# Two layers of linear attention and MLP on one core: 64 bytes more in an unused tile

## The chip, the cores and the metric

The kernel runs on one core of a Trainium2 chip. The metric is the device time of one execution in microseconds. The profile is taken from a single execution by the hardware profiler; its span runs from the first to the last instruction of the program.

## The reference

Two layers, each an attention block without softmax followed by an MLP, over 2048 rows of 448 columns in float32 (16 heads of 28):

```
phi = lambda t: jnp.where(t > 0, t + 1, jnp.exp(t)) + 1e-6
def A(x, wqkv, wo):
    q, k, v = heads(x @ wqkv)
    kv = einsum("bhsd,bhse->bhde", phi(k), v)
    z  = einsum("bhsd->bhd", phi(k))
    o  = einsum("bhqd,bhde->bhqe", phi(q), kv) / (einsum("bhqd,bhd->bhq", phi(q), z) + 1e-6)
    return merge(o) @ wo
def B(x, w1, b1, w2, b2):
    return gelu(x @ w1 + b1) @ w2 + b2      # 448 -> 1792 -> 448
for layer in range(2):
    x = x + A(layernorm(x), wqkv, wo)
    x = x + B(layernorm(x), w1, b1, w2, b2)
```

## The kernel before

Precision: each large product is made of float32r matmuls. An operand is split into a high part (a cast copy by ACT) and a low part (the rest, by DVE or POOL), and the product is high x high, high x low and low x high, all added into the same PSUM bank. Of the last 64 of the 448 rows of a contraction, high and low parts are stacked into one operand of 128 partitions, so that two matmuls do instead of three.

Staging: a layer has two parts. Phase 1 goes over 16 tiles of 128 rows: layer norm, transpose, the k and q projections (`proj`, L306 to L311), phi, and the accumulation of G (L481 to L485, normalised x against phi(k), four banks). A transition then forms z, the kv matrix and its product with wo (L621, L641, L651), in plain float32. Phase 2 goes over four blocks of four tiles. For each of 14 slices of 128 hidden columns, `mlp1` makes the first MLP product: 11 matmuls that write 128 x 512 (L801 to L805); slices of w1 are stationary and the block's normalised, transposed x (`XH`, `XL`) is moving. ACT makes g by gelu and gh by a cast copy, DVE gl. `mlp2` makes the second product: for each of the block's four tiles 3 matmuls that write 128 x 448 (L819 to L821); gh or gl is stationary and a slice of w2 is moving. The attention part of the next block is put between (L743 to L747 among it).

A matmul of TensorE is preceded by a weight load of its own: the stationary operand's 128 columns are read from SBUF (row PEld, LDWEIGHTS), and then the moving operand's columns are read and streamed through.

Order: the kernel is written under a manual schedule, so each engine's instructions stand in the order of the program; TensorE works through one list.

Memory: tiles come from pools and are given addresses in SBUF in the order in which their tags are first used, one behind the other. The address is the byte offset within each of the 128 partitions. What matters here, in order, with the start of the first buffer modulo 256 bytes as the built program has it:

- pool `consts` (`ones` and `ident` at 128), pool `wts`: w1h, w1l, w1x, w2h, w2l, all at 64; their slices begin at multiples of 256 bytes from there
- pool `work`, first tags: nine x tiles at 64, five halves `S` of 4096 bytes at 64 (staging, transposed squares, Mh and part of Ml), the twelve small tiles of the layer norm's statistics (bst, bmv, bve, brs, 32 bytes each)
- the unused tile `space`, L912, 128 bytes
- then `tail`, the tags W (wk, pq and others), `XH`, `XL`, V (wq), A (gh, qh, xnh), B (gl, ql, xnl), e (g, phi), E and F (kh, kl, qh, ql), xn, and the small dn and rd. All of these but the small ones start at 64 modulo 256.

Nothing ever writes or reads `space`; it sets where the tiles behind it lie. The lines around it:

```
    stage_a(0, 0)
    work.tile([128, 32], F32, name="space", tag="space", bufs=1)
    bn = ln_bn(xt[0, 1])
    stage_n(0, 0)
```

`stage_a` is what first allocates the statistics' tiles, `stage_n` what first allocates `tail`.

Of the kernel before, what the change touches and what calls it, by code (L numbers as in the profile page):

```python
# [9 lines left out]
F32 = mybir.dt.float32  # L10
# [12 lines left out]
def linear_attn_mlp_kernel(  # L23
# [28 lines left out]
    work = ctx.enter_context(tc.tile_pool(name="work", bufs=2))  # L52
# [138 lines left out]
    def ln_bn(xs):  # L191
        st = work.tile([128, 6], F32, name="bst", tag="bst", bufs=3)
        dve.bn_stats(st, xs)  # L193
        return st
# [182 lines left out]
    def stage_a(l, t):  # L377
        sts[l, t] = ln_stats(xt.pop((l, t)))
# [530 lines left out]


    stage_a(0, 0)
    work.tile([128, 32], F32, name="space", tag="space", bufs=1)  # L912
    bn = ln_bn(xt[0, 1])
    stage_n(0, 0)
    split_hi("k", 0, st_k)
# [4 lines left out]
    for l in range(LAYERS):  # L920
# [27 lines left out]
        for tok in ORDER.split():  # L948
            name, j = tok.rstrip("0123456789"), int("0" + tok.lstrip("abcdefghijklmnopqrstuvwxyzQTG"))
# [69 lines left out]
```

## Time and profile before

| | us |
|---|---|
| median of 3 runs | 878.83 (878.70 to 878.84) |
| the profiled execution's own time | 877.81 |
| its span | 876.1 |
| TensorE: matmuls busy, in the span | 870.8 |
| first MLP product (L801 to L805), 1232 matmuls, start to start | 281.5 |
| second MLP product (L819 to L821), 1344 matmuls, start to start | 272.3 |
| other float32r matmuls, start to start | 291.3 |

The first three rows are measured times. In a profile, PE is TensorE's matmul stream and PEld its weight loads, which run beside it. Matmuls overlap in their pipeline, so the duration of one (365 ns at 448 columns, 391 ns at 512) is longer than the distance between two starts (about 203 and 227 ns); for the rate of the stream the distance counts. "Start to start" in the table is the sum of these distances over all matmuls of the lines named.

### The profile page before, as it was taken

To read this page: it belongs to the slowest core of one execution; us is meant where nothing else is said; L and a number is where in the kernel's file an instruction comes from. 1 tells how busy PE (TensorE), PEld (TensorE's weight loads), DVE (VectorE), ACT (ScalarE), POOL (GpSimd) and SP (SyncE) were. 2 spreads that over 40 slices of the span, in tenths; PEclk is the share of its full clock that TensorE was granted. 3 is DMA by queue.
4 is the path that set the end of the run, shared out by engine and by line. 5 is a ranking of instruction groups with operands and counts; after the bars stand their busy time and mean duration, and the time that the engine had idled before them with its cause. 6 is when DMAs were issued, how large, how long until landed. Compare 5 with 4: busy or idle time off the path is not lost.

```text
span 876.1 us, 11676 instructions
## 1 busy us (share of the span) xinstructions
PE 870.8 (99%) x4182; PEld 771.5 (88%) x4182; DVE 489.0 (56%) x953; ACT 343.3 (39%) x603; POOL 220.8 (25%) x250
## 2 busy tenths in 40 slices
PE   9999999999999999999999999999999999999998
PEld 8999888888888888888899998888888888888887
DVE  6877585658455443226477875864674483433112
ACT  5676635324323322333356565332233133223221
POOL 5566532335013102012222344110220140140000
PEclk9999999999999999999999999999999999999999
DMA  5475636633413402051146543352332423111001
GB/s 159 134 228 173 198 88 207 188 96 122 132 59 105 156 0 97 1 179 49 48 135 195 164 128 106 103 181 81 109 110 91 128 76 115 49 49 42 1 1 43
DMA packets 63482, 94.76 MB, mean 108 GB/s; under 512 B 8896, under 2 KB 58560, under 8 KB 63424
## 3 DMA queue, kind: packets, MB, share of 16 engines
q1 hardware_dynamic: 63424, 94.01, 34.5%
q8 instruction: 33, 0.54, 0.3%
q14 instruction: 25, 0.20, 0.1%
HBM read 56.17 MB, written 34.60 MB: 104 GB/s over the span
## 4 chain that ended last, share of the span: by engine, by line
PE 98%; DVE 0%; DMA 0%; POOL 0%; ACT 0%; issue 0%; DVEq 0%
PE y L821 10%; PE y L819 10%; PE y L820 10%; PE hp L802 9%; PE hp L803 9%; PE hp L801 9%; PE hp L805 3%; PE hp L804 3%; PE psk L307 2%; PE G L482 2%; PE psq L306 2%; PE psq L307 2%; PE psq L308 2%; PE G L481 2%; PE G L483 2%; PE psk L308 2%
## 5 line engine op out<-in xcount | busy, mean ns | idle before, releaser
L811 DVE TENSOR_TENSOR gl<-g,gh 128x512 fp32r<-128x512 f32 x112 | 83.4, 745 | 299.8 <-ACT gh L810 299.8
L807 ACT ACTIVATE g<-hp,b1s 128x512 f32<-128x512 f32 x112 | 77.1, 689 | 406.5 <-PE hp L805 403.3
L821 PE MATMUL y<-w2h,gl 128*128 128x448 f32 x448 | 163.7, 365 | 0.0
L820 PE MATMUL y<-w2l,gh 128*128 128x448 f32 x448 | 163.6, 365 | 0.0
L819 PE MATMUL y<-w2h,gh 128*128 128x448 f32 x448 | 163.6, 365 | 0.0
L802 PE MATMUL hp<-XH,w1l 128*128 128x512 f32 x336 | 131.5, 391 | 0.0
L801 PE MATMUL hp<-XH,w1h 128*128 128x512 f32 x336 | 131.2, 391 | 0.0
L803 PE MATMUL hp<-XL,w1h 128*128 128x512 f32 x336 | 131.2, 391 | 0.0
L203 POOL TENSOR_TENSOR brs<-bve,mhalf 128x1 f32<-128x1 f32 x64 | 39.5, 618 | 284.6 <-DVE bve L201 276.5
L819 PEld LDWEIGHTS y<-w2h,gh 128*128 128x128 f32 x448 | 84.1, 188 | 9.0
L820 PEld LDWEIGHTS y<-w2l,gh 128*128 128x128 f32 x448 | 84.1, 188 | 8.4
L821 PEld LDWEIGHTS y<-w2h,gl 128*128 128x128 f32 x448 | 84.2, 188 | 6.6
L803 PEld LDWEIGHTS hp<-XL,w1h 128*128 128x128 f32 x336 | 63.1, 188 | 14.1 <-issue 0.6
L802 PEld LDWEIGHTS hp<-XH,w1l 128*128 128x128 f32 x336 | 63.1, 188 | 11.3
L801 PEld LDWEIGHTS hp<-XH,w1h 128*128 128x128 f32 x336 | 63.1, 188 | 10.9
L810 ACT CAST gh<-g 128x512 fp32r<-128x512 f32 x112 | 69.6, 622 | 3.6
L694 POOL TENSOR_TENSOR pz<-pq,zb 128x448 f32<-128x448 f32 x32 | 36.7, 1150 | 87.2 <-DVE dn L700 71.3
L416 POOL TENSOR_TENSOR xnl<-x,xnh 128x384 fp32r<-128x384 f32 x32 | 35.1, 1097 | 70.0 <-ACT xnh L415 37.9
L296 DVE TENSOR_TENSOR XL<-sp,XH 128x512 fp32r<-128x512 f32 x50 | 42.9, 864 | 4.2 <-ACT XH L295 4.2
L805 PE MATMUL hp<-XL,w1x 128*128 128x512 f32 x112 | 43.6, 389 | 0.0
L804 PE MATMUL hp<-XH,w1x 128*128 128x512 f32 x112 | 43.6, 389 | 0.0
L193 DVE BATCH_NORM_STATS2 bst<-x 128x6 f32<-128x448 f32 x64 | 39.9, 624 | 4.8 <-DMA x<-in_A_x_dram 3.7
(146 smaller groups left out, 1565.0 us busy)
## 6 DMA issues: line engine op xcount, KB each, us to landing
x<-in_A_x_dram SPq DMA_DIRECT2D x32, 224.0 KB, 3.8
pq_d<-eq SPq DMA_DIRECT2D x32, 224.0 KB, 2.9
pq<-pq_d SPq DMA_DIRECT2D x32, 224.0 KB, 3.3
sq_m<-sq SPq DMA_DIRECT2D x14, 512.0 KB, 2.8
sp<-sq_m SPq DMA_DIRECT2D x56, 128.0 KB, 3.1
x<-x_d SPq DMA_DIRECT2D x32, 224.0 KB, 3.4
sq_a<-sq SPq DMA_DIRECT2D x12, 512.0 KB, 2.9
sp<-sq_a SPq DMA_DIRECT2D x48, 128.0 KB, 3.1
```

Of the source, the lines that this page charges most:

```text
L296: eng.tensor_tensor(lo.rearrange("p (c i n) -> p c i n", c=4, n=32), x, f(h), op=OP.subtract)
L801: pe.matmul(o, w1h[:, c, s], x.moving(x.hi, c), start=(c == 0), stop=False)
L802: pe.matmul(o, w1l[:, c, s], x.moving(x.hi, c), start=False, stop=False)
L803: pe.matmul(o, w1h[:, c, s], x.moving(x.lo, c), start=False, stop=False)
L804: pe.matmul(o, w1x[:, s], x.moving(x.hi, 3), start=False, stop=False)
L805: pe.matmul(o, w1x[:, s], x.moving(x.lo, 3), start=False, stop=True)
L807: act.activation(g, hp, AF.Gelu_apprx_tanh, bias=b1s[:, i:i + 1])
L810: act.copy(gh, g)
L811: dve.tensor_sub(gl, g, f(gh))
L819: pe.matmul(acc[j], gh[:, s], w2h[:, i], start=first, stop=False)
L820: pe.matmul(acc[j], gh[:, s], w2l[:, i], start=False, stop=False)
L821: pe.matmul(acc[j], gl[:, s], w2h[:, i], start=False, stop=last)
```

## The change

The unused tile takes 192 bytes of each partition and not 128. Every tile that is allocated behind it lies 64 bytes higher; tiles before it (w1, w2, the x tiles, the halves, the statistics) stay. Those that started at 64 modulo 256 behind the tile start at 128.

```
     stage_a(0, 0)
-    work.tile([128, 32], F32, name="space", tag="space", bufs=1)
+    work.tile([128, 48], F32, name="space", tag="space", bufs=1)
     bn = ln_bn(xt[0, 1])
```

## The prediction

> **What bounds the kernel now.** I read the page's busy times first, then the chain that ended last, then the groups, then TensorE's timeline.
>
> ```profile
> PE 870.8 (99%) x4182; PEld 771.5 (88%) x4182; DVE 489.0 (56%) x953; ACT 343.3 (39%) x603; POOL 220.8 (25%) x250
> ```
> ```profile
> PE 98%; DVE 0%; DMA 0%; POOL 0%; ACT 0%; issue 0%; DVEq 0%
> ```
> ```profile
> L821 PE MATMUL y<-w2h,gl 128*128 128x448 f32 x448 | 163.7, 365 | 0.0
> L802 PE MATMUL hp<-XH,w1l 128*128 128x512 f32 x336 | 131.5, 391 | 0.0
> L821 PEld LDWEIGHTS y<-w2h,gl 128*128 128x128 f32 x448 | 84.2, 188 | 6.6
> ```
>
> TensorE is busy 870.8 of 876.1 us, and 98% of the chain is matmuls that wait for nothing: no transfer, no other engine. The granted clock is 0.999. So only the rate of the matmul stream can move the end. Its means (365 and 391 ns) overlap and are not that rate; the distance from one start to the next is. In the timeline (columns: start us, duration us, engine, line, operation):
>
> ```profile
> 427.25 0.36 PE L819 MATMUL y<-w2h,gh 128*128 128x448 f32 x1
> ...
> 429.47 0.37 PE L821 MATMUL y<-w2h,gl 128*128 128x448 f32 x1
> 429.68 0.39 PE L801 MATMUL hp<-XH,w1h 128*128 128x512 f32 x1
> ```
> ```profile
> 427.25 0.19 PEld L820 LDWEIGHTS y<-w2l,gh 128*128 128x128 f32 x1
> 427.45 0.19 PEld L821 LDWEIGHTS y<-w2h,gl 128*128 128x128 f32 x1
> ```
>
> Twelve matmuls of the second MLP product take 2.43 us, 202.5 ns each. Each one's successor has its weights loaded from the moment it starts (427.25 and 427.25), for 188 ns: during every matmul, TensorE reads two SBUF streams side by side, the moving operand of this one and the stationary operand of the next. Their addresses are what the change touches.
>
> The same kind of stream does not always run at that rate. These are two passages of phase 1 with the same sequence of lines, 20 matmuls of 448 columns from G's L481 to psq's L310, first in layer 0, then in layer 1:
>
> ```profile
> 98.71 0.37 PE L481 MATMUL G<-kh,xnh 128*128 128x448 f32 x1
> 98.91 0.37 PE L482 MATMUL G<-kl,xnh 128*128 128x448 f32 x1
> ...
> 102.84 0.37 PE L310 MATMUL psq<-wq,XH 128*128 128x448 f32 x1
> ```
> ```profile
> 528.93 0.36 PE L481 MATMUL G<-kh,xnh 128*128 128x448 f32 x1
> 529.14 0.36 PE L482 MATMUL G<-kl,xnh 128*128 128x448 f32 x1
> ...
> 532.99 0.36 PE L310 MATMUL psq<-wq,XH 128*128 128x448 f32 x1
> ```
>
> 20 steps take 4.13 us in the first (206.5 ns each) and 4.06 us in the second (203.0). In nanoseconds the first is a steady 207, 207, 206 (mean 206.7), the second repeats 199, 207, 202, 203, 202 (mean 202.7). The slower rate holds from 10 to 16, 36 to 42 and 93 to 114 us; a passage changes over only where a stall or a transpose has shifted the phase. In the stretches' table the clock is 1.00 in both kinds. So the two streams of reads have more than one stable way to run beside each other, 4.0 ns apart, with everything at the same address modulo 256.
>
> **The change, part by part.** It adds and removes no instruction; the built programs have the same rows on all five engines. In the allocations, the 128-byte tile before and the 192-byte tile after stand behind the small tiles, so all SBUF tiles allocated later lie 64 bytes higher. Before, w1, w2, the x tiles, the staging halves, XH, XL, wk, wq, gh and gl all start at 64 modulo 256. After, w1, w2, x and the halves stay at 64, and XH, XL, wk, wq, gh and gl go to 128.
>
> Which pairs change: the first MLP product, 1232 matmuls (w1 stationary at 64, XH or XL moving at 128), and the second, 1344 (gh or gl stationary at 128, w2 moving at 64). The projections, G, and the o products of later blocks have both operands above the tile and keep their relation, 0; block 0's o products (96 matmuls, L732 to L734) change but are worth at most 96 x 4.0 ns = 0.4 us, left out.
>
> DVE, ACT, POOL and DMA addresses move too. I cost that at nothing: they are hidden under matmuls that wait 0.0, and DVE, the busiest, is 56% busy. Were the cover gone, a 1% slower DVE would be 4.9 us in all; nothing in the page puts one of its instructions on the path but the last four adds (2.45 us together).
>
> Start to start, summed over the trace: the first product takes 281.5 us (mean 228.5 ns), the second 272.3 us (202.7 ns). No row shows a stream of these matmuls with another relation, so each is bounded from both sides by the spacings seen.
> - Second product, 448 columns. Seen singly: 199 to 207 ns; sustained: 202.7 or 206.7. Bounds: 1344 x (199 - 202.7) = -5.0 us and 1344 x (206.7 - 202.7) = +5.3 us. The nearest instance is the last psq matmul (L311, moving at 64) beside the load of `ones` (at 128), the relation that the second product will have: in the two layers 202 and 206 ns. That is within what the relation 0 shows, and a little above its mean. I take +5.3 us: the sustained spacing other than today's is the slower one, and no stretch is sustained below 202.7.
> - First product, 512 columns. Steady 226.7 in every group of eleven, with the first three (or five, after a projection) at 230 to 236, then back:
>
> ```profile
> 603.22 0.40 PE L802 MATMUL hp<-XH,w1l 128*128 128x512 f32 x1
> 603.46 0.39 PE L803 MATMUL hp<-XL,w1h 128*128 128x512 f32 x1
> 603.69 0.40 PE L801 MATMUL hp<-XH,w1h 128*128 128x512 f32 x1
> ```
>
> Bounds: none of the slow first ones, 1232 x (226.7 - 228.5) = -2.2 us, or all at the least seen, 224: -5.5 us; all like the first three (231, 233, 231, mean 231.7): 1232 x 3.2 = +4.0 us, or all at 236: +9.3 us. I take 0, since no second steady spacing is seen for it.
>
> Sum: 877.81 us (the profiled execution's own time, 876.1 of it span) + 5.3 = 883.1. The median of the runs, 878.83, is 1.0 above the profiled one, so the forecast is 884.1, say 884.
>
> One rule of the skill speaks against any effect. The Trainium skill ("SBUF — State Buffer", section "Who interferes with whom") gives TensorE two independent read ports, one for the moving operand and one for the loads, and says that TensorE never waits on anyone. By it the sum would be 0 and the time 878.8. The two spacings above do not refute that, as they show one stream's rate changing and not who is in whose way.
>
> **The rivals.**
> - *Faster.* If, with equal addresses, the two streams meet at the same place at the start of each matmul and 64 bytes keep them apart, part of what each matmul takes beyond its columns goes. For it: the short members of the patterns, 199 and 224; in the float32 products of the transition the first matmul, whose next load is at the same address modulo 256, takes 380 ns and the seven behind it 375 or 376, most of them with loads elsewhere (though the first of a group is often slow). Against it: in the kv products (L641), spacing stays 98 ns where the next load lies 64 bytes away. Without slow entries and with the second product at 199: 878.8 - 2.2 - 5.0 = 871.6; with the first at 224: 868.3. The Trainium skill ("TensorE: Matmul & The Clock Gate", "Wait — 56ns, not 53.3ns?") has 215.7 ns between bf16 matmuls of 512 columns, 11 ns under the steady 226.7 here; by an estimate from that figure the first product alone would save 1232 x 12.8 ns = 15.7 us, for 863.
> - *No change.* Reads of the two operands do not meet, or they sweep past each other at different speeds and meet as often from any start; then the two spacings come from the phase alone. For it: the 98 ns of L641, and 202 and 206 at the one matching pair. Against it: the phase alone, a nanosecond or two at the entry, already chooses between spacings 2% apart. Time 878.8.
> - *Both products slower.* The first product stays in its entry state too: 884.1 + 4.0 = 888.1, at its largest spacing 893.4. It decides from the point where the fourth matmul of a group is still above 228.
> - *The change doesn't do what it says:* excluded by the allocations for the addresses.
>
> **How the numbers follow.** A measurement of this kernel (878.70 to 878.84) can tell 0.2%, 1.8 us, from no change. Slower through the second product or both: 0.54, of which 0.34 for the second alone, the forecast of 884, and 0.20 for both. Faster: 0.32. No change: 0.14. So faster 0.32, same 0.14, slower 0.54. The forecast's own range, with both products, is 880.6 to 893. As the faster case holds a third of the chance, the range reaches to its lower bound: 868 to 893. Outside I leave 0.07 below (spacings under any seen here) and 0.10 above (a worse meeting than any in this trace).
>
> **What would show it.** Right: L819 to L821 start 206 to 207 ns apart in every group of twelve (2.48 us instead of 2.43), weight loads still 188 ns and starting with the matmul, phase 1 with the same two spacings as now. Wrong: groups of twelve at 2.39 us or groups of eleven at 2.49 us or less (the faster rival); both as they are, 2.43 and 2.51 (no change); longer weight loads, or a wait of TensorE on another engine, would mean a mechanism that I have not named.

## The result, and the profile after

The changed kernel takes 883.88 us (median of 4 runs, 883.84 to 884.62) against 878.84 before (878.70 to 878.95): ratio 1.0059, 95% interval 1.0042 to 1.0077. The forecast of 884.0 was met, but most of the working behind it was not, as the profile shows.

The page of the changed kernel, busy times and the chain that ended last:

```profile
PE 876.3 (99%) x4182; PEld 771.5 (87%) x4182; DVE 490.0 (56%) x953; ACT 343.6 (39%) x603; POOL 221.8 (25%) x250
PE 95%; DMA 2%; DVE 1%; ACT 1%; issue 1%; SPq 0%; POOL 0%; DVEq 0%; ACTq 0%; POOLq 0%
```

TensorE is still the bound: 5.5 us more busy in a span that is 6.0 us longer (882.1), at granted clock 1.0 and with weight loads of the same total (771.5). The few per cent of other engines in the chain come mostly from two waits in phase 1 of layer 0, where TensorE is briefly ahead of DVE: from there the chain is followed back through DVE, ACT and transfers, but TensorE itself waits only 0.5 and 0.2 us (waits of TensorE on others, changed kernel: us in total, times, longest):

```profile
PE psq L306 <- DVE eq L320: 0.5, 1, 0.5
PE G L482 <- DVE kl L440: 0.2, 1, 0.2
```

Waits like these are not owed to the new addresses: the last experiment below, whose tiles behind the unused one keep before's places modulo 256, has the same wait of 0.5 us, and the first has that of 0.2.

The groups of the two MLP products after the change (busy us, mean ns of one):

```profile
L819 PE MATMUL y<-w2h,gh 128*128 128x448 f32 x448 | 164.2, 367 | 0.0
L821 PE MATMUL y<-w2h,gl 128*128 128x448 f32 x448 | 162.9, 364 | 0.0
L820 PE MATMUL y<-w2l,gh 128*128 128x448 f32 x448 | 162.2, 362 | 0.0
L803 PE MATMUL hp<-XL,w1h 128*128 128x512 f32 x336 | 132.8, 395 | 0.0
L801 PE MATMUL hp<-XH,w1h 128*128 128x512 f32 x336 | 132.0, 393 | 0.0
L802 PE MATMUL hp<-XH,w1l 128*128 128x512 f32 x336 | 131.2, 390 | 0.0
```

Lines that were alike before now differ: L819, L820 and L821 all had 365, and have 367, 362 and 364. Before, L820 and L819 stood beside the L821 of the prediction with:

```profile
L820 PE MATMUL y<-w2l,gh 128*128 128x448 f32 x448 | 163.6, 365 | 0.0
L819 PE MATMUL y<-w2h,gh 128*128 128x448 f32 x448 | 163.6, 365 | 0.0
```

That is not a uniform slowdown but another pattern of long and short steps. The timeline of one group of eleven and the twelve that follow, changed kernel:

```profile
437.32 0.39 PE L801 MATMUL hp<-XH,w1h 128*128 128x512 f32 x1
...
439.62 0.40 PE L805 MATMUL hp<-XL,w1x 128*128 128x512 f32 x1
439.86 0.36 PE L819 MATMUL y<-w2h,gh 128*128 128x448 f32 x1
...
442.29 0.37 PE L819 MATMUL y<-w2h,gh 128*128 128x448 f32 x1
```

Eleven matmuls of the first product take 2.54 us and twelve of the second 2.43, as before. The eleven took 2.51 us before, from the L801 at 429.68 in the prediction's rows to the next product's first matmul:

```profile
432.19 0.36 PE L819 MATMUL y<-w2h,gh 128*128 128x448 f32 x1
```

And this is phase 1 of layer 1, the passage of the prediction, from G's L481 to psq's L310:

```profile
533.37 0.37 PE L481 MATMUL G<-kh,xnh 128*128 128x448 f32 x1
...
537.50 0.37 PE L310 MATMUL psq<-wq,XH 128*128 128x448 f32 x1
```

20 steps in 4.13 us, 206.5 ns each, where before took 203.0 there. Nothing in this passage has changed its relation: both operands lie above the tile.

The start-to-start times, summed over the two profiled executions (the program's last matmul has no next start, so the second product has 1343 steps):

| part | before, us | after, us | difference |
|---|---|---|---|
| first MLP product, 1232 matmuls | 281.46 (228.5 ns) | 284.48 (230.9 ns) | +3.02 |
| second MLP product, 1343 steps | 272.28 (202.7 ns) | 271.82 (202.4 ns) | -0.46 |
| o products of blocks 1 to 3 (L743 to L747) | 53.42 (202.3 ns) | 54.20 (205.3 ns) | +0.78 |
| phase 1, layer 1 | 91.40 | 93.20 | +1.80 |
| phase 1, layer 0 | 102.13 | 103.30 | +1.17 |
| the two transitions | 70.12 | 69.82 | -0.30 |
| all | 870.81 | 876.81 | +6.0 |

The profiled execution of before is 1.0 us under its median and that of after at its median; the 1.17 us of phase 1 of layer 0 are about that difference. That phase took 102.1, 102.8 and 102.9 us in three kernels that differ in nothing there (before, and two of the experiments), so its line tells little.

### The profile page after: what moved, and what is told of

It is laid out like the page before. It is cut to its first block, busy times and chain, and to the rows that moved or that the text cites. A ratio compares the mean times of both kernels' runs of the same rounds, so it can differ in the third digit from the quotient of the medians.

```text
span 882.1 us, 11676 instructions
## 1 busy us (share of the span) xinstructions
PE 876.3 (99%) x4182; PEld 771.5 (87%) x4182; DVE 490.0 (56%) x953; ACT 343.6 (39%) x603; POOL 221.8 (25%) x250
## 4 chain that ended last, share of the span: by engine, by line
PE 95%; DMA 2%; DVE 1%; ACT 1%; issue 1%; SPq 0%; POOL 0%; DVEq 0%; ACTq 0%; POOLq 0%
PE y L819 10%; PE y L821 10%; PE y L820 10%; PE hp L803 9%; PE hp L801 9%; PE hp L802 9%; PE hp L805 3%; PE hp L804 3%; PE psq L306 2%; PE psq L307 2%; PE psq L308 2%; PE psk L307 2%; PE psk L308 2%; PE G L482 2%; PE psk L306 2%; PE G L483 2%
## 5 line engine op out<-in xcount | busy, mean ns | idle before, releaser
L819 PE MATMUL y<-w2h,gh 128*128 128x448 f32 x448 | 164.2, 367 | 0.0
L821 PE MATMUL y<-w2h,gl 128*128 128x448 f32 x448 | 162.9, 364 | 0.0
L820 PE MATMUL y<-w2l,gh 128*128 128x448 f32 x448 | 162.2, 362 | 0.0
L801 PE MATMUL hp<-XH,w1h 128*128 128x512 f32 x336 | 132.0, 393 | 0.0
L820 PEld LDWEIGHTS y<-w2l,gh 128*128 128x128 f32 x448 | 84.1, 188 | 9.2
L819 PEld LDWEIGHTS y<-w2h,gh 128*128 128x128 f32 x448 | 84.1, 188 | 8.2
L821 PEld LDWEIGHTS y<-w2h,gl 128*128 128x128 f32 x448 | 83.8, 187 | 7.8
L801 PEld LDWEIGHTS hp<-XH,w1h 128*128 128x128 f32 x336 | 63.1, 188 | 10.5
L763 POOL TENSOR_TENSOR x<-x,b2b 128x448 f32<-128x448 f32 x32 | 42.0, 1333 | 0.0
```

Source lines behind the costliest of these rows:

```text
L801: pe.matmul(o, w1h[:, c, s], x.moving(x.hi, c), start=(c == 0), stop=False)
L819: pe.matmul(acc[j], gh[:, s], w2h[:, i], start=first, stop=False)
L820: pe.matmul(acc[j], gh[:, s], w2l[:, i], start=False, stop=False)
L821: pe.matmul(acc[j], gl[:, s], w2h[:, i], start=False, stop=last)
```

## The experiments

Each kernel was timed beside the kernel before, which took 878.3 to 878.9 us in these sessions; each ratio is to the time beside it. Theory R: the rate of a matmul stream follows its relation, the distance modulo 256 between its moving operand and the stationary operand that is loaded beside it. Rivals: any shift of tiles lays out the run anew (L); and, for the parts whose relation has not changed, the phase at entry (P). "Phase" stands for the point of its repeating pattern of steps at which a stream begins; it is inferred from the steps, as no view shows it.

A third rival is that the other engines or the transfers, whose tiles have moved too, hold TensorE up. The trace of the changed kernel answers it. Its 84 groups of eleven that stand between two groups of the second product take 2536 or 2537 ns each, whatever runs beside them, so it is not the other engines or the transfers that make them longer. Two of them, the first with DVE busy for 2.44 us, POOL for 2.40 and the transfers at 0.48, the second with DVE, ACT, POOL and the transfers all at nothing:

```profile
152.01:154.55 2.54, 2.54 (x12) 2.06 (x11) 2.44 (x5) 0.00 (x0) 2.40 (x2) 1.00 0.48 100
845.91:848.44 2.53, 2.53 (x12) 2.07 (x11) 0.00 (x0) 0.00 (x0) 0.00 (x0) 1.00 0.00 0
```

(The columns are the stretch, its length, the busy time and count of PE, PEld, DVE, ACT and POOL, the granted clock, the share of the transfers and their GB/s.)

**The unused tile at 384 bytes.** Everything behind it 256 bytes higher than before.

```
-    work.tile([128, 32], F32, name="space", tag="space", bufs=1)
+    work.tile([128, 96], F32, name="space", tag="space", bufs=1)
```

> Unused tile of 384 bytes: all tiles behind it lie 256 bytes higher than before, so every relation modulo 256 is as before. Theory R (the rate of a matmul stream follows the distance, modulo 256, between its moving operand and the stationary operand loaded beside it): 878.8 us, first product 228.5 ns a matmul, second 202.7, phase 1 of layer 1 at 202.7. Rival L (any shift of the upper tiles lays out the run anew): a time unlike before's by some us, like after's 883.9 or elsewhere.

Measured: 878.78 us, ratio 1.0003 (0.9994 to 1.0012). First product 228.4 ns a matmul, second 202.8, phase 1 of layer 1 91.41 us. A shift of 256 bytes is no change, so a shift as such is not what counts; L falls.

**w1 alone, w2 alone, both.** The upper tiles keep their places modulo 256; the weights move to 0 with gaps ahead and behind (here both; for w1 alone the second gap, 64 bytes, stands ahead of w2h, for w2 alone the first, 192 bytes, does).

```
-    w1h = wts.tile([128, 3, F], F32R, name="w1h")
+    wts.tile([128, 48], F32, name="gap0", tag="gap0", bufs=1); w1h = wts.tile([128, 3, F], F32R, name="w1h")
...
-    w2l = wts.tile([128, NF, D], F32R, name="w2l")
+    w2l = wts.tile([128, NF, D], F32R, name="w2l"); wts.tile([128, 16], F32, name="gap1", tag="gap1", bufs=1)
```

> Only w1h, w1l, w1x are shifted, to 0 modulo 256, with 192 bytes ahead of them and 64 behind; XH and XL stay at 64, all else keeps its place modulo 256. The first product has after's relation (moving 64 above stationary), nothing else changes. Theory R: first product 230.9 ns (+3.0 us), second near 202.7, 881.5 to 882 us, if its exit does not choose another spacing elsewhere. Rival L (it is the place of the upper tiles that counts): 878.8, since these stay where they were modulo 256.

> Only w2h and w2l are shifted, to 0 modulo 256 (192 bytes ahead, 64 behind); the second product has after's relation (moving 64 below stationary), nothing else changes. Theory R: second product 202.4 ns or near it (-0.5 us), with after's pattern of 207, 199, 201; the end of the second product enters phase 1 of layer 1 in another phase, and if that chooses the 206.7 ns spacing there, +1.9 us: 880.2 us; if it does not, 878.4. Rival L: 878.8 with before's pattern 199, 207, 202, 203, 202.

> w1 and w2 both at 0 modulo 256, all upper tiles at 64 as before: both relations as in after, at other addresses. Theory R: 883.9 us as after, first product 230.9 ns, second 202.4, phase 1 of layer 1 at 206.7. Rival L: 878.8. If first and second product are as in after but phase 1 is not: 882 us, and the rest of after's loss is the entry's phase and not the relation.

| | time, us | ratio (95%) | first product, ns | second, ns | phase 1 layer 1, us |
|---|---|---|---|---|---|
| w1 alone | 884.03 | 1.0061 (1.0048 to 1.0074) | 230.0 | 203.5 | 93.20 |
| w2 alone | 881.99 | 1.0038 (1.0024 to 1.0051) | 230.7 | 202.0 | 93.20 |
| both | 883.66 | 1.0056 (1.0044 to 1.0069) | 230.8 | 202.4 | 93.20 |

Both together are the changed kernel at other addresses, and its groups of matmuls come out to the nanosecond as after's do (the kernel with w1 and w2 moved):

```profile
L819 PE MATMUL y<-w2h,gh 128*128 128x448 f32 x448 | 164.2, 367 | 0.0
L821 PE MATMUL y<-w2h,gl 128*128 128x448 f32 x448 | 162.9, 364 | 0.0
L820 PE MATMUL y<-w2l,gh 128*128 128x448 f32 x448 | 162.2, 362 | 0.0
```

So the distances count, and it does not matter which of the tiles moves. But R is not the whole of it, as the parts do not add up: w1 alone costs +5.1 us and w2 alone +3.1, both +4.8, and the first two are more than was expected (881.5 to 882 us if nothing changed elsewhere, and at most 880.2). In the kernel with w2 alone the second product has become 1.0 us faster, and the loss is in the first product (+2.8 us) and phase 1 of layer 1 (+1.8), whose own relations are still 0. A group of eleven of it, from its first matmul to the first of the next product:

```profile
436.05 0.39 PE L801 MATMUL hp<-XH,w1h 128*128 128x512 f32 x1
436.28 0.40 PE L802 MATMUL hp<-XH,w1l 128*128 128x512 f32 x1
...
438.59 0.37 PE L819 MATMUL y<-w2h,gh 128*128 128x448 f32 x1
```

2.54 us. Start to start its steps are 232, 234, 235, 225, 230, 236, 229, 232, 231 and only then 227, 226; before they were 231, 232, 231 and then 227, 226 for the rest. It takes nine steps to settle and not three, 2537 ns a group against 2508: the first product pays for the way in which the second leaves TensorE. With w1 alone the first product's own relation shows: its steps settle at a repeating 229, 232, 226 (mean 228.9) where relation 0 settles at 226.7. There it is the second product, at its own relation 0, that pays 1.1 us: in about 30 of its 112 groups of twelve most or all steps are at 206.7 ns, the slower spacing that the prediction found in phase 1. One of them takes 2.47 us, from its first matmul to the first of the next product:

```profile
155.87 0.36 PE L819 MATMUL y<-w2h,gh 128*128 128x448 f32 x1
...
158.34 0.39 PE L801 MATMUL hp<-XH,w1h 128*128 128x512 f32 x1
```

So each product's rate depends on its own relation and on what the stream before it leaves.

**Other distances.** The unused tile at 256, 320 and 160 bytes (`[128, 64]`, `[128, 80]`, `[128, 40]`), that is, upper tiles 128 above, 64 below and 32 above the weights modulo 256.

> Unused tile of 256 bytes: XH, XL, gh, gl and all behind lie 128 bytes from w1 and w2 modulo 256. Theory R with four places of 64 bytes each: a third kind of pattern, unlike before's and after's; first product between 226 and 236 ns a matmul, second between 199 and 207, so 868 to 893 us by the bounds of before. A theory in which two places of 64 bytes alternate (period 128) gives before's pattern: 878.8 us.

> Unused tile of 320 bytes: the upper tiles lie 192 bytes above, that is 64 below, w1 and w2 modulo 256. The signs of after's relations are exchanged. If what counts is only that the streams do not start in the same place, as after: about 884 us; if the sign counts, the first product gets what the second has in after (short steps among long ones, mean no more than 228.5) and the other way round, time within 2 us of before.

> Unused tile of 160 bytes: the upper tiles lie 32 bytes above w1 and w2 modulo 256. If the places that matter are 64 bytes wide and a tile that straddles two of them behaves like a mixture, between before and after (879 to 884 us); if they are 32 bytes or finer, a pattern of its own; if only whole lines of 64 bytes count and the start is rounded down, before's patterns and 878.8 us.

| upper tiles minus weights, modulo 256 | time, us | ratio (95%) | first product, ns | second, ns | phase 1 layer 1, us |
|---|---|---|---|---|---|
| 0 (before) | 878.8 | 1 | 228.5 | 202.7 | 91.40 |
| 32 | 887.55 | 1.0104 (1.0090 to 1.0117) | 232.8 | 204.3 | 93.19 |
| 64 (after) | 883.88 | 1.0059 (1.0042 to 1.0077) | 230.9 | 202.4 | 93.20 |
| 128 | 884.92 | 1.0076 (1.0062 to 1.0089) | 232.2 | 203.8 | 91.42 |
| 192 | 884.32 | 1.0065 (1.0052 to 1.0077) | 233.4 | 201.2 | 93.20 |

Every distance has patterns of its own: the period is neither 64 nor 128, and 32 is no mixture of 0 and 64 but the slowest. At 192 bytes the time is the 884 us expected if it only counts that the streams do not start in the same place, but 32 bytes take 887.55 us, and each distance gives the parts another time, so that reading does not hold. The expectation that exchanging the signs exchanges what the products take failed: at 192 the first product is at its slowest. What did come out is that the second product is at its fastest there, with w2 lying 64 bytes above gh. None of these beats relation 0 as a whole, because the first product is fastest at 0.

**A kick at the entry of phase 1 of layer 1.** The changed kernel, and then the kernel before, with one matmul of 128 columns more, whose result the next one overwrites.

```
-        b = blocks[key]
-        for c in cs:
+        b = blocks[key]; kick = (name, key, j) == ('k', ('a', 1, 0), 0)
+        for c in (kick and pe.matmul(o[:, :128], b.still(b.hi, j, 0), wkq[name, 0][0][:, :128], start=True, stop=True), *cs)[1:]:
```

> The changed kernel with one matmul more, of 128 columns, ahead of the first k projection of layer 1 (the next matmul overwrites its result). No address changes. Theory P (in phase 1, where both operands have relation 0, the spacing is chosen by the phase at entry): the stream of 448 columns in phase 1 of layer 1 falls into 202.7 ns and not 206.7 there: 93.2 us become 91.6 with the 0.2 us of the added matmul, and the time 882.3 us; or the kick happens not to suffice and it stays at 884.1. Rival (phase 1 is slower because of the new addresses): 206.7 ns whatever the entry, 884.1 us.

> The kernel before with the same added matmul of 128 columns ahead of layer 1's first k projection; all addresses as before. Theory P (the spacing in phase 1 is chosen by the phase at entry, whatever the addresses): the entry that gave 202.7 ns is disturbed, and phase 1 of layer 1 either goes to 206.7 (+1.8 us and 0.2 for the matmul: 880.8) or, if this kick always leads to 202.7, stays (879.0). Rival (before's addresses hold it at 202.7): 879.0 always, so only 880.8 tells them apart.

The changed kernel with the kick: 881.92 us, ratio 1.0038 (1.0025 to 1.0051). Its timeline at the entry:

```profile
444.83 0.22 PE L303 MATMUL psk<-wk,XH 128*128 128x128 f32 x1
444.89 0.42 PE L306 MATMUL psk<-wk,XH 128*128 128x448 f32 x1
445.15 0.37 PE L307 MATMUL psk<-wk,XH 128*128 128x448 f32 x1
...
449.00 0.36 PE L310 MATMUL psq<-wq,XH 128*128 128x448 f32 x1
449.20 0.36 PE L311 MATMUL psq<-wq,XL 128*128 128x448 f32 x1
```

From 445.15 to 449.20 are 20 steps in 4.05 us, 202.5 ns each, and the phase takes 91.52 us: the 91.40 of before and 0.12 for the kick, at the addresses of after. So the 1.8 us of phase 1 come from its entry and not from its addresses. The three kernels with weights moved say the same from the other side: there the tiles of phase 1 keep before's places modulo 256, and it takes 93.20 us all the same. The kernel before with the kick stays at 202.7 ns there and at 878.66 us (1.0001, 0.9992 to 1.0010); this kick leads to the fast spacing from both sides, so that run does not tell the theories apart.

**w2 the other way.** As w2 alone, but 64 bytes ahead of w2h and 192 behind w2l, so that w2 lies 64 above gh and gl.

> As the third experiment, but w2h and w2l go to 128 modulo 256 instead of 0 (64 bytes ahead, 192 behind): the second product has its moving operand 64 bytes above gh and gl, the relation of the sixth run, where it took 201.2 ns a matmul. Own relation alone counting: 1343 x 1.5 ns less than before, 876.7 us. If, as in the third experiment, the first product pays for leaving another phase behind (more slow matmuls at the start of each eleven, about 2.8 us) and phase 1 of layer 1 goes to 206.7 (1.8 us): 881.3 us.

Measured: 876.75 us against 878.51, ratio 0.9978 (0.9969 to 0.9987): faster than both kernels. Its groups:

```profile
L821 PE MATMUL y<-w2h,gl 128*128 128x448 f32 x448 | 162.6, 363 | 0.0
L820 PE MATMUL y<-w2l,gh 128*128 128x448 f32 x448 | 162.5, 363 | 0.0
L819 PE MATMUL y<-w2h,gh 128*128 128x448 f32 x448 | 162.1, 362 | 0.0
```

Start to start the second product takes 200.7 ns a matmul (-2.7 us); the first pays 0.9 us for its entry (229.2 ns, five slow steps in each eleven); phase 1 of layer 1 keeps its 91.4 us. -2.7 + 0.9 is the 1.8 us gained.

## Why the prediction came out, by its own steps

- *What bounds the kernel: right.* The end moved with the matmul stream alone; weight loads kept 188 ns, the clock 1.0, and the other engines' new addresses cost nothing that shows. (The chain of before also passes through a few DVE instructions of the start-up, and not only through the last four adds; nothing hangs on it.)
- *The change of relation alters the rate: right,* and shown by the shift of 256 bytes (1.0003) and by the same patterns at other addresses. The rival of no effect falls: the same instructions take between 200.7 and 204.3 ns, and between 228.4 and 233.4, when only the places of their operands change. The Trainium skill ("SBUF — State Buffer", section "Who interferes with whom") says that TensorE's two read ports are independent and that it never waits on anyone, by which there would be no effect; the measurement differs, and it decides. Whether the two reads themselves hold each other up, no run shows.
- *Second product, +5.3 us: wrong.* The step that failed is "I take +5.3 us: the sustained spacing other than today's is the slower one". 206.7 is a spacing of relation 0 and says nothing of another relation; the product became 0.46 us shorter (202.4 ns a matmul). The two single steps at the new relation (202 and 206 ns) could not tell, since the steps of one group go from 199 to 207; their mean, 204, is 1.6 ns above what came.
- *First product, 0: wrong,* +3.0 us. The step that failed is "I take 0, since no second steady spacing is seen for it". It has another steady pattern at the new relation (228.9 ns against 226.7 in the kernel with w1 alone), and more of its steps are slow at the entry when the second product has changed (nine against three with w2 alone). The bound of +4.0 us, given as "all like the first three", held.
- *Phase 1, o products: left out.* "The projections, G, and the o products of later blocks ... keep their relation" is true, and the prediction itself said that the entry's phase chooses between 202.7 and 206.7. It did not ask what phase the changed products would leave to them. That was worth +1.8 us (shown by the kick) and +0.8 us. These o products take 205.3 ns also with w1 and w2 both moved, where their own tiles keep before's places modulo 256, so it is not their addresses; that it is their entry is argued and was not tried by itself.
- *The sum: right by luck.* +5.3 was to come from the second product alone; in its place -0.5 (second product) + 3.0 (first) + 1.8 (phase 1 of layer 1) + 0.8 (o products) make 5.1. What held on its own merit is the range, read from the steps of the stream.
- *Its signs: not met.* Right was to be groups of twelve at 2.48 us, and they stayed at 2.43; the groups of eleven went to 2.54, with a fourth step of 236 ns, which was the sign of "Both products slower", while the second product was not slower. None of the named cases came as described.
- *The faster rival* had a true core: another relation can be faster, as with w2 64 bytes above gh (200.7 ns), but it is not the one that the change makes for both products.

## What to carry to other kernels

Where TensorE is the bound and each matmul loads its own weights, the place of the moving operand against the stationary one modulo 256 bytes is worth up to 1% here (878.8 to 887.6 us, float32r), and a shift of 32 bytes already counts. An unused tile sets it. It is tried for each pair of tiles, and judged by the whole kernel's time: w2 moved one way made its own product faster and the kernel 3.1 us slower, and the other way the kernel 1.8 us faster. Read the rate from start to start, step by step, never from the mean duration. A part whose own operands have not moved can still change, because its rate also depends on how the stream enters it.

## What the runs showed of the hardware that was not expected

- A stream of equal float32r matmuls at equal relation showed two sustained spacings, 202.7 and 206.7 ns at 448 columns. One short matmul at its entry, which adds 0.12 us, moved the changed kernel's 93.20 us of phase 1 to 91.52.
- A shift of 256 bytes changes nothing that the runs can tell (878.78 against 878.89 us), and one of 128 does (884.92 against 878.32).
- Stays open: what in SBUF or TensorE has this period, why 32 bytes are the worst of those tried, and which phase leads to which spacing. The runs show the patterns and that the operands' places and the entry choose them, not the cause behind.
